# VectorE's score tiles as TensorE tasks of their own, and PV products that no longer wait for a full burst

## The chip, the cores and the metric

One core of one Trainium2 chip. The metric is device microseconds (us) of one execution. Every kernel was timed in several rounds beside the kernel before on the same chip, so a ratio compares runs of the same rounds. The granted TensorE clock differed from run to run. "Clock" below is always this granted share of full speed.

## The reference, cut to what matters

Two transformer layers over 2048 tokens of width 512, each an attention block and an MLP block with residuals. Attention has 32 heads of 16, and its softmax over 2048 keys is most of the work.

```python
B, S, D, H, Dh, F = 1, 2048, 512, 32, 16, 1376
q, k, v = qkv(layernorm(x) @ wqkv)                    # [32 heads, 2048, 16] each
p = softmax((q @ k.T) * Dh ** -0.5, axis=-1)          # 32 x 2048 x 2048
x = x + merge(p @ v) @ wo
x = x + gelu_tanh(layernorm(layernorm(x)) @ w1 + b1) @ w2 + b2
# ... and both lines once more
```

## The kernel before

The program is written by a list scheduler that runs at build time. Every piece of work is a `Task(engine, priority, instructions)`. The scheduler holds a model of when engines and buffers come free and emits each engine's instructions once, in one order. On the chip each engine then runs its own list in that order. Priorities therefore don't exist at run time: only the order and the waits do.

A score tile is 128 keys by 512 queries, in one PSUM bank. Two engines turn scores into weights:

- ScalarE (ACT) takes the exponential of three banks (0 to 2), then of two (3 and 4), and so on in turn.
- VectorE (DVE) takes single tiles in banks 5 (`DLANE`) or 7 (`MISCB`): it evicts the bank to integers whose bits are a rough exponential, makes three shifted copies, and all four images enter the PV product, three of them against pre-scaled copies of V.

Bank 6 (`ACCB`) accumulates PV. A head has 16 channels, so a score matmul uses one of four 32-row groups of TensorE's array (`hp` below). Matmuls in different row groups run side by side (further down, four take 0.39 us together, as long as one). I call a "pass" the time of one matmul, in which up to four such matmuls can run.

This is where a group's scores are sent; the tiles of VectorE (`dts`) join the same burst:

```python
# flow_scores
dts = []
while self.wide and len(grp) + len(dts) < 4:
    d = self.take_d([row groups already used by grp and dts])     # cut
    if d is None:
        break
    dts.append(d)
ops = []
for (sg, j), b in zip(grp, banks):
    ops.append(self.score(sg, j, b))
for sg, j, b, bt, w in dts:
    ops.append(self.score(sg, j, b))
...
yield Task("pe", 0.0, ops)
...                                    # submit the exponential of grp
for d in dts:
    self.d_load(d)                     # submit the eviction

# take_d(hps): a tile in a free row group if there is one
j = next((j for j in sg["todod"] if sg["tiles"][j][1] not in hps), sg["todod"][0])

# score: the row group is in tile_position
e.matmul(self.ps[:, b, ...], lhsT=self.KT[32 * hp:32 * hp + 32, ...],
         rhs=self.QT[32 * hp:32 * hp + 32, ...], tile_position=(32 * hp, 0))
```

PV products wait until a burst is worth its passes, here unless exponential buffers have run out:

```python
# try_pv
value = lambda r: sum(min(r, len(v)) for v in by.values()) / (4.0 * (r + PV_COST))
r = max(range(1, PV_DEEP + 1), key=value)
if value(r) < PV_LEAST and not self.starved and len(near) < sg["n"] - sg["sub"]:
    return
```

Where TensorE would be idle, `fill_pe` puts matmuls on zeros, as many as keep a running activity at `FILL_ACT = 0.62`. They are meant to keep the clock up: with fillers half as wide it was 0.963 to 0.973 (after_fillhalf below). It also sends a single VectorE tile if the gap is long enough, so tiles alone exist before the change too.

## Time and profile before

| | before |
|---|---|
| median of 3 runs (range) | 1710.54 us (1710.01 to 1712.83) |
| span of the profiled run, clock | 1708.6 us, 0.983 |
| ACT busy, idle | 1609.6 us, 99.0 us |
| TensorE matmul busy, idle | 1585.4 us, 123.2 us |
| tiles by ACT / by DVE | 3338 / 758 |
| passes of score matmuls, counted in the order | 1487 |
| filler matmuls of 256 columns | 6152 |

Idle time is the span less the busy time. The lines behind the table are in the prediction. One more of the page is needed later: the chain that ended last, by line, as shares of the span.

### The profile page before, as it was taken

What the parts mean: (1) busy time and instruction counts of PE and PEld (TensorE: products, weight loads), DVE (VectorE), ACT (ScalarE), POOL (GpSimd) and SP (SyncE); (2) the same over time, 40 slices, a digit from 0 to 9 for tenths busy, and PEclk for the clock granted to TensorE, in tenths of its full rate; (3) what the DMA queues carried; (4) which work ended last, traced back from release to release, by engine and by line L of the source; (5) the groups of instructions that cost most, each with busy time, mean ns of one, the idle gap of its engine ahead of it and who ended that gap; (6) DMA issues with size and microseconds to landing.
All of it is one profiled execution on the core that took longest, in us unless ns stands there. A gap on an engine that the chain in (4) does not pass through costs nothing.

```text
span 1708.6 us, 46394 instructions
## 1 busy us (share of the span) xinstructions
PE 1585.4 (93%) x19711; PEld 568.6 (33%) x19711; DVE 1374.4 (80%) x3011; ACT 1609.6 (94%) x1426; POOL 378.5 (22%) x640
## 2 busy tenths in 40 slices
PE   8988999999999999999999998999999999999998
PEld 5222333233223223332223333323232233344444
DVE  6878998859876798768878799886888869887783
ACT  4878999999999999999999999999999999999996
POOL 4045522102211121101212133411011101132220
PEclk9989999999999999999899999999999999999999
DMA  6552000112101120112532230000000100010000
GB/s 167 104 103 69 26 12 8 47 43 59 33 17 41 40 73 14 29 28 69 117 54 54 56 87 18 17 20 11 14 8 8 20 15 5 5 21 7 19 10 14
DMA packets 181259, 66.70 MB, mean 39 GB/s; under 512 B 160859, under 2 KB 175424, under 8 KB 181056
## 3 DMA queue, kind: packets, MB, share of 16 engines
q1 hardware_dynamic: 181056, 63.75, 16.6%
q8 instruction: 158, 2.59, 0.6%
q14 instruction: 45, 0.37, 0.1%
HBM read 19.96 MB, written 15.30 MB: 21 GB/s over the span
## 4 chain that ended last, share of the span: by engine, by line
PE 47%; ACT 40%; DVE 8%; POOL 2%; issue 2%; DMA 1%; SPq 0%; DVEq 0%; POOLq 0%
ACT PT L1110 37%; PE ps L1127 15%; PE ps L1278 13%; PE ps L1035 4%; PE ps L841 4%; PE ps L1397 4%; DVE dp L1195 3%; PE ps L1364 3%; PE ps L1435 3%; ACT h L1427 2%; DVE dp L1223 2%; POOL vs L986 1%; DVE accT L1304 1%; PE ps L1038 1%; ACT L1110 1%
## 5 line engine op out<-in xcount | busy, mean ns | idle before, releaser
L1110 ACT ACTIVATE PT<-ps 128x1536 bf16<-128x1536 f32 (+1 forms) x1348 | 1534.3, 1262 | 67.0 <-PE ps L1127 61.3
L1127 PE MATMUL ps<-QT,KT 32*128 32x512 bf16 (+1 forms) x4608 | 604.2, 363 | 108.5 <-ACT PT L1110 43.8
L1195 DVE TENSOR_SCALAR dp<-ps 128x512 uint16<-128x512 f32 x758 | 510.2, 682 | 208.4 <-PE ps L1127 200.7
L1278 PE MATMUL ps<-PT,V 128*17 128x512 bf16 (+1 forms) x3751 | 469.7, 363 | 0.4 <-DVE accT L1304 0.4
L1223 DVE TENSOR_SCALAR dp<-dp 128x1024 uint16<-128x1024 uint16 (+1 forms) x1170 | 443.2, 422 | 12.7 <-PE ps L1278 8.2
L986 POOL TENSOR_SCALAR vs<-V 128x340 bf16<-128x340 bf16 (+3 forms) x312 | 255.7, 826 | 859.7 <-PE ps L1278 833.1
L1278 PE MATMUL ps<-dp,vs 128*17 128x512 bf16 (+1 forms) x2571 | 397.3, 359 | 0.0
L1127 PEld LDWEIGHTS ps<-QT,KT 32*128 32x128 bf16 x4608 | 163.4, 91 | 637.8 <-issue 173.3
L1035 PE MATMUL ps<-wqkv,zw 128*32 128x256 bf16 x6152 | 241.5, 280 | 1.1 <-DVE accT L1304 1.1
L1278 PE MATMUL ps<-dp,V 128*17 128x512 bf16 (+1 forms) x857 | 201.4, 364 | 3.0 <-DVE accT L1304 2.9
L1035 PEld LDWEIGHTS ps<-wqkv,zw 128*32 128x32 bf16 x6152 | 144.5, 97 | 93.3 <-issue 76.0
L1278 PEld LDWEIGHTS ps<-PT,V 128*17 128x17 bf16 x3751 | 114.7, 88 | 91.1 <-issue 73.7
L1278 PEld LDWEIGHTS ps<-dp,vs 128*17 128x17 bf16 x2571 | 101.9, 89 | 85.3 <-issue 71.4
L1397 PE MATMUL ps<-yT,wf 128*128 128x512 bf16 (+3 forms) x396 | 98.5, 359 | 0.5 <-DVE h L1421 0.3
L841 PE MATMUL ps<-wqkv,xnT 128*128 128x512 bf16 x336 | 94.2, 389 | 2.9 <-DVE dp L862 2.1
L1304 DVE STREAM_TRANSPOSE accT<-ps 128x512 f32<-128x512 f32 (+1 forms) x88 | 58.3, 662 | 24.4 <-PE ps L1278 22.9
L1421 DVE TENSOR_SCALAR h<-ps,b1c 128x512 bf16<-128x512 f32 (+2 forms) x88 | 62.0, 705 | 13.9 <-PE ps L1397 13.5
L1364 PE MATMUL ps<-wo,OT 128*128 128x512 bf16 x240 | 67.4, 383 | 0.2
L1278 PEld LDWEIGHTS ps<-dp,V 128*17 128x17 bf16 x857 | 48.9, 88 | 38.4 <-issue 24.3
L906 POOL TENSOR_TENSOR qt<-n,qy 128x32 f32<-128x32 f32 x32 | 11.1, 347 | 160.1 <-DVE qy L902 159.6
L1344 DVE STREAM_TRANSPOSE OT<-ob 128x512 bf16<-128x512 bf16 (+1 forms) x72 | 46.0, 640 | 0.2
L1397 PEld LDWEIGHTS ps<-yT,wf 128*128 128x128 bf16 (+1 forms) x396 | 29.5, 99 | 46.5 <-issue 18.6
(154 smaller groups left out, 820.1 us busy)
## 6 DMA issues: line engine op xcount, KB each, us to landing
wf<-in_B_w_dram SPq DMA_DIRECT2D x90, 128.0 KB, 2.8
q_scr<-qk SPq DMA_DIRECT2D x22, 256.0 KB, 2.1
k_scr<-qk SPq DMA_DIRECT2D x12, 256.0 KB, 2.0
out_dram<-xres SPq DMA_DIRECT2D x16, 128.0 KB, 1.7
v_scr<-vst SPq DMA_DIRECT2D x12, 136.0 KB, 2.0
V<-v_scr SPq DMA_DIRECT2D x8, 204.0 KB, 4.5
wqkv<-in_A_wqkv_dram SPq DMA_DIRECT2D x3, 512.0 KB, 3.9
q_scr<-h SPq DMA_DIRECT2D x6, 256.0 KB, 2.1
```

What stands on the lines that cost most here:

```text
L841: yield Task("pe", prio, [I(lambda e, c=c: e.matmul(self.ps[:, b, :], lhsT=xnT[:, c, :], rhs=self.wqkv[:, c, which * 512:which * 512 + 512 ...
L986: yield Task("pool", 0.8, [I(lambda e, k=k: e.tensor_scalar(out=self.vs[:, q, k - 1, i:i + n, :], in0=src, scalar1=WSHIFT[k], scalar2=None ...
L1035: P.op("pe", lambda e, p=p: e.matmul(self.ps[p:p + 32, b, 0:w], lhsT=self.zw[:, 0:32], rhs=rhs[:, 0:w], start=st, stop=st, skip_group_chec ...
L1110: S_.submit(Task("act", 1e-5 * gi, [I(lambda e, pt=pt, n=n, b0=b0: e.activation(out=self.PT[:, pt:pt + n, :], in_=self.ps[:, b0:b0 + n, :] ...
L1127: return [I(lambda e, kb=kb, i=i: e.matmul(self.ps[:, b, i * W:(i + 1) * W], lhsT=self.KT[32 * hp:32 * hp + 32, hg, kb * 128:(kb + 1) * 12 ...
L1195: self.S_.submit(Task("dve", 0.0, [I(lambda e: e.tensor_scalar(out=self.dp[:, u, w * 512:(w + 1) * 512], in0=self.ps[:, b, :], scalar1=BIT ...
L1223: yield Task("dve", pr, [I(lambda e, k=k, v=v: e.tensor_scalar(out=self.dp[:, v, 0:N], in0=self.dp[:, u, 0:N], scalar1=float(SHIFT[k]), sc ...
L1278: ops.append((i, I(lambda e, hp=hp, v=v, ap=ap[:, i * W:(i + 1) * W], first=first and i == 0, W=W: e.matmul(self.ps[32 * hp:32 * hp + 17, ...
L1304: yield Task("dve", 0.3, [I(lambda e: e.transpose(self.accT[:, a, 0:W], self.ps[:, ACCB, 0:W]), [("ps", ACCB)], [RA], 0.15 + 0.53 * W / 512)])
L1364: yield Task("pe", pr, [I(lambda e, hg=hg, i=i, b=b: e.matmul(self.ps[:, b, :], lhsT=self.OT[:, hg, i * 128:(i + 1) * 128], rhs=self.wo[:, ...
L1397: yield Task("pe", pr, [I(lambda e, c=c: e.matmul(self.ps[0:M, b, off:off + W], lhsT=self.w1(fc, c), rhs=self.yT[:, c, 0:W], start=(c == 0 ...
L1421: S_.submit(Task("dve", pr - 0.7, [I(lambda e, fc=fc, M=M, b=b: e.tensor_scalar(out=hv[0:M, fc * W:(fc + 1) * W], in0=self.ps[0:M, b, 0:W] ...
```

## The change

The intent: a VectorE tile should not have to wait for an ACT group, and VectorE should get one whenever it is about to run out of work; PV products that wait for partners should go if TensorE has nothing else. The diff, cut to its core:

```diff
+D_IDLE = 1.0
+D_PRIO = 0.5
+PV_IDLE = 0.4
@@ flow_scores
-            for sg, j, b, bt, w in dts:
-                ops.append(self.score(sg, j, b))
+            for d in dts:
+                S_.submit(Task("pe", -0.5, self.score(d[0], d[1], d[2])), cb=lambda d=d: self.d_load(d))
...
-            for d in dts:
-                self.d_load(d)
@@ new
+    def d_solo(self):
+        S_ = self.S_
+        if not self.wide or self.P.free["dve"] - S_.now + sum(o[4] for t in S_.pend["dve"] for o in t.ops) > D_IDLE:
+            return
+        d = self.take_d([])
+        if d is not None:
+            S_.submit(Task("pe", D_PRIO, self.score(d[0], d[1], d[2])), cb=lambda: self.d_load(d))
@@ d_loaded: a timer at the planned end of each eviction calls d_solo
+        heapq.heappush(S_.timers, (self.P.last_writer[("dp", bt["unit"], w)].t1, S_.seq, self.d_solo))
@@ try_pv
             if value(r) < PV_LEAST and not self.starved and len(near) < sg["n"] - sg["sub"]:
-                return
+                t = self.P.drain + PV_IDLE
+                if S_.now < t or self.pv_out:
+                    ...                # set a timer for pv_again, which calls try_pv
+                    return
```

More of the change, by code (lines that the diff above doesn't have):

```diff
@@ L1204, in d_loaded @@
             self.S_.release("mb", b)
+        S_ = self.S_
+        S_.seq += 1
+        heapq.heappush(S_.timers, (self.P.last_writer[("dp", bt["unit"], w)].t1, S_.seq, self.d_solo))
         self.d_ready(bt, 0, bt["unit"], [w])
@@ L1259, in try_pv @@
             if value(r) < PV_LEAST and not self.starved and len(near) < sg["n"] - sg["sub"]:
-                return
+                t = self.P.drain + PV_IDLE
+                if S_.now < t or self.pv_out:
+                    if not self.pv_timer:
+                        self.pv_timer = True
+                        S_.seq += 1
+                        heapq.heappush(S_.timers, (max(t, S_.now) + 0.01, S_.seq, self.pv_again))
+                    return
             pick = [v[k] for k in range(r) for v in by.values() if len(v) > k]
@@ L1284, in try_pv, with pv_again @@
             S_.submit(Task("pe", 1.0, ops), cb=lambda sg=sg, pick=pick: self.pv_done(sg, pick))
+    def pv_again(self):
+        self.pv_timer = False
+        self.try_pv()
     def pv_done(self, sg, pick):
@@ L1531, in build @@
         self.pv_first = False
+        self.pv_timer = False
         self.starved = False
```

## The prediction

> **What bounds the kernel now.** I read the page's busy shares and chain first, then busy time by stage, then the groups by shape, then the waits of ScalarE (ACT). A score tile is a 128x512 block of logits in one PSUM bank. Most go to ACT, which takes the exponential of three or two banks in turn. Some go to VectorE (DVE): it evicts the bank to integers (L1195), makes three shifted copies (L1223), and all four images enter the PV product.
>
> ```profile
> PE 1585.4 (93%) x19711; PEld 568.6 (33%) x19711; DVE 1374.4 (80%) x3011; ACT 1609.6 (94%) x1426; POOL 378.5 (22%) x640
> ...
> PE 47%; ACT 40%; DVE 8%; POOL 2%; issue 2%; DMA 1%; SPq 0%; DVEq 0%; POOLq 0%
> ```
>
> PE and ACT both look full. But PE's 93% holds filler matmuls on zeros (L1035), and TensorE's ends are modelled. The stages separate them:
>
> ```profile
> core 0: us, PE busy (x) PEld busy (x) DVE busy (x) ACT busy (x) POOL busy (x), PEclk, DMA share, GB/s
> 0.00:200.00 200.00, 177.07 (x1813) 68.05 (x1816) 154.79 (x366) 155.63 (x158) 86.52 (x238) 0.94 0.45 100
> 200.00:1600.00 1400.00, 1309.02 (x16314) 450.08 (x16306) 1148.00 (x2478) 1362.79 (x1183) 276.08 (x384) 0.99 0.14 32
> 1600.00:1709.00 109.00, 99.36 (x1600) 50.44 (x1592) 71.57 (x170) 91.20 (x87) 15.86 (x18) 1.00 0.06 13
> ```
>
> For 1400 us ACT works 97.3% of the time: idle is 37 us there, 44 us in the start and 18 us in the tail. What ACT still waits for in the middle is one thing:
>
> ```profile
> ACT PT L1110 <- PE ps L1127: 31.8, 85, 1.8
> ```
>
> That is 85 short waits for score matmuls, 0.37 us each. So the kernel is ACT-bound, and time is bought by taking tiles from ACT without making it wait longer. The shapes give the price of a tile, the DVE side and the filler:
>
> ```profile
> L1110 ACT ACTIVATE PT<-ps 128x1536 bf16<-128x1536 f32 x642 | 953.9, 1486 | 43.2 <-PE ps L1127 38.2
> L1110 ACT ACTIVATE PT<-ps 128x1024 bf16<-128x1024 f32 x706 | 743.8, 1059 | 23.8 <-PE ps L1127 23.1
> L1195 DVE TENSOR_SCALAR dp<-ps 128x512 uint16<-128x512 f32 x758 | 510.2, 682 | 208.4 <-PE ps L1127 200.7
> L1223 DVE TENSOR_SCALAR dp<-dp 128x1024 uint16<-128x1024 uint16 x1104 | 427.7, 429 | 12.5 <-PE ps L1278 8.2
> L1035 PE MATMUL ps<-wqkv,zw 128*32 128x256 bf16 x6152 | 241.5, 280 | 1.1 <-DVE accT L1304 1.1
> ```
>
> One more bank costs ACT 1486 - 1059 = 427 ns. DVE is idle 208 us ahead of its evictions, nearly all of it waiting for a score matmul: that is the idle time the change goes after.
>
> **What the Trainium skill says.** "ScalarE: Activation LUTs", section "What ACT_TABLE_LOAD costs": an ACTIVATE with immediate operands is 186 ns plus 0.833 ns per column, and neighbours overlap by about 93 ns. 512 columns are 427 ns; the trace agrees. The two forms sum to 1697.7 us but cover 1534.3 us together, an overlap of 121 ns per instruction, so one instruction's fixed cost is 1059 - 854 - 121 = 84 ns.
> "TensorEngine Tiling (Array Packing)", section "Key Properties": changing the tiling mode drains TensorE. In the timeline, bursts inside one mode start 0.22 us apart (802.88 to 803.10), across modes 0.32 us (804.39 to 804.71): a switch costs about 0.1 us.
> "PSUM — Partial Sum Buffer", section "Engine vs sequencer instructions": ACT and DVE queues are strict FIFO and matmuls start and end in program order. The trace agrees, painfully, just after the kernel widens to five banks:
>
> ```profile
> 108.29 0.41 DVE L782 TENSOR_SCALAR xn<-xres,mv,rs 128x512 bf16<-128x512 bf16 x1 [7.16 <-DMA xnT<-xn]
> ...
> 109.74 1.03 PE L1127 MATMUL ps<-QT,KT 32*128 32x512 bf16 x4 [6.94 <-DVE dp L1195]
> ...
> 110.87 2.54 ACT L1110 ACTIVATE PT<-ps 128x1536 bf16<-128x1536 f32 x2 [6.23 <-PE ps L1127]
> ```
>
> A late DMA held DVE, the bank DVE had not emptied held PE, and PE starved ACT.
>
> **The change, part by part.** The scheduler runs at build time, so I compared the two instruction orders. DMA and GpSimd counts are equal. ACT loses 13 of the 1536-wide and 14 of the 1024-wide exponentials and gains one of 512: 3338 tiles become 3272. DVE evictions go from 758 to 824, wide shifts from 1104 to 1215, narrow ones from 66 to 42. By units of eight head groups the gain is 13 tiles at most (92 to 105) and 1 to 10 in the others, so it is spread over the middle.
>
> ACT: 66 tiles x 0.427 = 28.2 us, plus 26 fewer instructions x 0.084 = 2.2 us: 30.4 us less. All of it lies on the bounding engine.
>
> DVE: 66 x 0.673 (510.2/758) = 44 us, 111 x 0.387 (427.7/1104) = 43 us, less 24 x 0.26 = 6 us: busy 1374 to about 1455 us, 87% of a 1680 us span. It fits into the 208 us of idle time and is off the bounding path.
>
> PE: each tile that moves needs four PV products in place of one: 198 more tile products, four at a time in the 0.22 us of the timeline, about 11 us. Score passes: for each run of adjacent score matmuls I took the longest queue on one 32-row group. That gives 1487 passes before and 1887 after. The old code put a DVE tile into the ACT group's burst and chose a free row group; a solo tile has no such choice or stands alone. 400 x 0.22 = 88 us more. PV passes count 1762 before and 1827 after, 65 x 0.22 = 14 us, so the smaller bursts waste little beyond the 11 us. Mode switches rise from 2687 to 2798, 111 x 0.1 = 11 us. Fillers of this kind fall from 6152 to 4432, 430 passes of four x 0.11 (256 columns, half a pass) = 47 us less. Net PE work: 88 + 14 + 11 - 47 = +66 us, in a span that should be 30 us shorter. It lies beside ACT's work as long as each ACT group finds its banks written in time, but the slack goes: filler (1538 x 0.11 = 169) plus idle (1708.6 - 1585.4 = 123) is about 292 us before and roughly 292 - 113 - 30 = 149 us after.
>
> PV while idle: PV never bounds ACT directly in this trace (no listed ACT wait names it); earlier products free exponential buffers sooner. I count nothing for it.
>
> Sum with ACT idle unchanged: 1710.5 - 30.4 = 1680.1 us.
>
> **Rivals.**
> (1) PE becomes the co-bound. With half its slack gone, more groups come late. For: solo tiles stand ahead of PV in priority, the tiles taken with a group now even ahead of that group, and I count 135 runs of score matmuls that open with a tile in a DVE bank ahead of an ACT group, against 63 before; in such a run a late DVE holds ACT up at once. Against: groups still outrank everything but those tiles, the new code no longer makes a group wait for DVE's bank to be planned free, and ACT has 1.0 to 1.4 us of other banks to chew on. If the 85 waits doubled, 32 us come back: about 1710, no gain at all. I expect about a tenth of that.
> (2) ACT's idle time shrinks. PE's score matmuls wait 29.2 us on DVE evictions in the middle; if decoupling removes a third of ACT's 32 us and the 6.2 us stall at 110 us, the result is near 1664. Against: that stall starts from a late DMA that the change does not touch, and the changed order still has DVE wait there for the same kind of transfer and PE wait for several.
> (3) DVE becomes the bound. At 87% with FIFO waits it would show as later eviction and fewer free banks. Against: the scheduler stops giving it tiles when it has over 1.3 us queued. It would make the time about 1690.
> (4) Fewer fillers let the clock fall. Granted clock is 0.99 in the middle; real work replaces the fillers, so I expect no change.
>
> **Range and chances.** From 1680 I add 2 us for rival 1 in part offset by 2: 1682 us, 1.7% under 1710.5. The range takes ACT idle from 8 us less to 14 us more: 1672 to 1694. The line for faster by 2% is 1676.3 us; it needs the full tile saving and 4 us less idle: 0.24. Slower by 2% needs over 64 us of new waits: 0.01. Within 2%: 0.75.
>
> **What would show it right or wrong.** Right: exponentials 1503 to 1505 us busy on the page, DVE near 1455, ACT busy near 1579 and ACT idle within 10 us of 99, most of it still in the first 200 us; fillers 4432. Step by step: if ACT busy falls by 30 but the span by less, the wait list must show ACT waiting for score matmuls for much more than 61 us over the whole span, and rival 1 (PE waits on evictions grow) or 3 is read from what those matmuls waited for. If the span falls by over 34 us, those waits must be well under 61 us. The prediction is wrong in kind if ACT is under 96% busy between 200 and 1570 us, or the granted clock there falls under 0.97.

## More of the kernel before

L1110 is the exponential, L1127 the score matmul, L1278 the PV product, L1035 the filler.

```profile
ACT PT L1110 37%; PE ps L1127 15%; PE ps L1278 13%; PE ps L1035 4%; PE ps L841 4%; PE ps L1397 4%; DVE dp L1195 3%; PE ps L1364 3%; PE ps L1435 3%; ACT h L1427 2%; DVE dp L1223 2%; POOL vs L986 1%; DVE accT L1304 1%; PE ps L1038 1%; ACT L1110 1%
```

The chain runs through ACT's exponentials for 37% of the span and through TensorE's score and PV work for 28%.

## The result, and the profile after

| | before | after |
|---|---|---|
| median, range | 1710.28 us (1708.60 to 1712.83) | 1694.92 us (1691.75 to 1697.68) |
| ratio (95%) | | 0.9908 (0.9884 to 0.9933) |
| profiled span, clock | 1708.6, 0.983 | 1695.3, 0.988 |
| ACT busy / idle | 1609.6 / 99.0 | 1580.9 / 114.4 |
| DVE busy | 1374.4 | 1456.1 |
| TensorE busy / idle | 1585.4 / 123.2 | 1618.0 / 77.3 |

A ratio here and below is the mean time of one kernel's runs over that of the other's of the same rounds, so it is not quite the ratio of the medians quoted. The change gains 0.9%: within 2%, as expected, but little more than half of the 28.5 us predicted, and the median lies 0.9 us above the predicted range.

First the page of the kernel after: busy time by engine, then the chain that ended last by engine and by line. L1113 is now the exponential, L1128 the score matmul, L1297 the PV product.

```profile
PE 1618.0 (95%) x18235; PEld 543.4 (32%) x18235; DVE 1456.1 (86%) x3164; ACT 1580.9 (93%) x1400; POOL 384.0 (23%) x640
...
PE 60%; ACT 30%; DVE 6%; DMA 2%; issue 1%; SPq 1%; POOL 0%; DVEq 0%; POOLq 0%
ACT PT L1113 27%; PE ps L1128 22%; PE ps L1297 17%; PE ps L844 4%; PE ps L1420 4%; PE ps L1458 4%; PE ps L1038 4%; PE ps L1387 3%; DVE dp L1205 2%; DVE dp L1236 2%; ACT h L1450 2%; PE ps L1041 1%; DMA yT<-xn 1%; DVE accT L1327 1%; DMA xnT<-xn 0%
```

The arithmetic of tiles came true: ACT works 28.7 us less. But the chain, which was 47% TensorE and 40% ACT, is now 60% and 30%, with score matmuls up from 15% to 22%. Busy shares alone hardly show this: TensorE goes from 93% to 95%.

The stages of the kernel after (columns as in the prediction's table of stages):

```profile
0.00:200.00 200.00, 181.82 (x1896) 69.93 (x1900) 161.03 (x371) 158.81 (x162) 87.24 (x241) 0.97 0.47 100
200.00:1590.00 1390.00, 1335.89 (x14879) 422.44 (x14868) 1222.62 (x2627) 1335.63 (x1157) 281.68 (x383) 0.99 0.14 33
1590.00:1695.30 105.30, 100.27 (x1469) 51.01 (x1467) 72.43 (x169) 86.41 (x83) 15.09 (x16) 0.99 0.04 12
```

In the middle ACT was busy for 97.3% and is for 96.1%: 54 us idle where 37 us were. Start and tail are as before (41 and 19 us idle). So the lost gain is in the middle. ACT's waits for score matmuls there, then TensorE's largest waits over the whole span, all in the kernel after (us in total, times, longest):

```profile
ACT PT L1113 <- PE ps L1128: 48.7, 78, 5.6
```
```profile
PE ps L1128 <- ACT PT L1113: 21.3, 76, 0.9
PE ps L1128 <- DVE dp L1205: 17.1, 22, 6.3
```

and TensorE's in the kernel before:

```profile
PE ps L1127 <- ACT PT L1110: 43.8, 133, 1.0
PE ps L1127 <- DVE dp L1195: 43.2, 69, 6.9
```

ACT waits more for TensorE (31.8 to 48.7 us in the middle), and TensorE waits less for ACT and for DVE, half or under half as long. An engine that others wait for longer while it waits less itself is the one short of time. Most of its lateness is then not a bank that is still full, but other work in front. That is a reading; the experiments have to test it.

What is that work? The score matmuls by shape, before and after; the number after the bar is busy time, and the idle time just before them follows.

```profile
L1127 PE MATMUL ps<-QT,KT 32*128 32x512 bf16 x3584 | 530.4, 389 | 97.9 <-ACT PT L1110 39.3 <-DVE dp L1195 38.5 <-DVE QT L969 2.8
```
```profile
L1128 PE MATMUL ps<-QT,KT 32*128 32x512 bf16 x3584 | 591.5, 384 | 49.2 <-ACT PT L1113 19.7 <-DVE dp L1205 15.6 <-DVE mv L773 2.3
```

The same 3584 matmuls of the same size keep TensorE busy for 61 us more; with the 1024 narrower ones it is 74 us (604.2 to 678.4). One matmul isn't longer (389 and 384 ns): fewer run side by side. The timeline shows it. A run of four score matmuls in the kernel before:

```profile
607.80 0.39 PE L1127 MATMUL ps<-QT,KT 32*128 32x512 bf16 x4
```

and in the kernel after, a run of four and the exponential that it released (start, duration, count, idle time before it):

```profile
604.57 0.61 PE L1128 MATMUL ps<-QT,KT 32*128 32x512 bf16 x4
605.06 7.09 ACT L1113 ACTIVATE PT<-ps 128x1536 bf16<-128x1536 f32 x6 [0.26 <-PE ps L1128]
...
606.51 0.60 PE L1128 MATMUL ps<-QT,KT 32*128 32x512 bf16 x4
```

Four in 0.39 us is one pass in four row groups; four in 0.6 us is two passes: one of the tiles shares a row group with another.

Where do the 400 added passes come from? Mostly not from tiles that stand alone. Counted over the two emitted orders, the runs of score matmuls without any ACT tile rise only from 13 to 67, while the passes that VectorE's tiles add to runs with ACT tiles rise from 122 to 489. Both kernels take 498 tiles together with a group and choose a row group that is free in it. Before, all of them stand in the burst of that group. After, as tasks of their own, 389 of them are emitted earlier, behind the group *before*, with whose row groups nobody compared them. These make about 340 of the 400 passes; the run at 604.57 us above is one, by its place in the order, while the one at 606.51 us holds a solo tile.

### The profile page after: what moved, and what is told of

Its sections match the earlier page's. It is cut to its first block, busy times and chain, and to the rows that moved or that the text cites. A ratio compares the mean times of both kernels' runs of the same rounds, so it can differ in the third digit from the quotient of the medians.

```text
span 1695.3 us, 43536 instructions
## 1 busy us (share of the span) xinstructions
PE 1618.0 (95%) x18235; PEld 543.4 (32%) x18235; DVE 1456.1 (86%) x3164; ACT 1580.9 (93%) x1400; POOL 384.0 (23%) x640
## 4 chain that ended last, share of the span: by engine, by line
PE 60%; ACT 30%; DVE 6%; DMA 2%; issue 1%; SPq 1%; POOL 0%; DVEq 0%; POOLq 0%
ACT PT L1113 27%; PE ps L1128 22%; PE ps L1297 17%; PE ps L844 4%; PE ps L1420 4%; PE ps L1458 4%; PE ps L1038 4%; PE ps L1387 3%; DVE dp L1205 2%; DVE dp L1236 2%; ACT h L1450 2%; PE ps L1041 1%; DMA yT<-xn 1%; DVE accT L1327 1%; DMA xnT<-xn 0%
## 5 line engine op out<-in xcount | busy, mean ns | idle before, releaser
L1113 ACT ACTIVATE PT<-ps 128x1024 bf16<-128x1024 f32 (+1 forms) x1322 | 1505.8, 1256 | 81.6 <-PE ps L1128 75.8
L1128 PE MATMUL ps<-QT,KT 32*128 32x512 bf16 (+1 forms) x4608 | 678.4, 359 | 53.1 <-ACT PT L1113 21.3
L1205 DVE TENSOR_SCALAR dp<-ps 128x512 uint16<-128x512 f32 x824 | 557.8, 684 | 121.2 <-PE ps L1128 114.0
L1236 DVE TENSOR_SCALAR dp<-dp 128x1024 uint16<-128x1024 uint16 (+1 forms) x1257 | 490.4, 432 | 10.9 <-PE ps L1297 6.6
L1297 PE MATMUL ps<-PT,V 128*17 128x512 bf16 (+1 forms) x3674 | 472.0, 361 | 0.2 <-DVE accT L1327 0.2
L1297 PE MATMUL ps<-dp,vs 128*17 128x512 bf16 (+1 forms) x2802 | 408.2, 357 | 0.4 <-DVE dp L1236 0.4
L1128 PEld LDWEIGHTS ps<-QT,KT 32*128 32x128 bf16 x4608 | 178.5, 91 | 578.7 <-issue 172.5
L1297 PE MATMUL ps<-dp,V 128*17 128x512 bf16 (+1 forms) x934 | 195.7, 358 | 2.4 <-DVE accT L1327 2.2
L1038 PE MATMUL ps<-wqkv,zw 128*32 128x256 bf16 x4432 | 188.2, 275 | 0.8 <-DVE accT L1327 0.8
L1297 PEld LDWEIGHTS ps<-PT,V 128*17 128x17 bf16 x3674 | 111.3, 88 | 114.9 <-issue 102.2
L1297 PEld LDWEIGHTS ps<-dp,vs 128*17 128x17 bf16 x2802 | 102.4, 89 | 111.2 <-issue 95.3
L1038 PEld LDWEIGHTS ps<-wqkv,zw 128*32 128x32 bf16 x4432 | 105.8, 96 | 80.3 <-issue 60.8
L1420 PE MATMUL ps<-yT,wf 128*128 128x512 bf16 (+3 forms) x396 | 104.8, 369 | 4.8 <-DMA yT<-xn 3.9
L1297 PEld LDWEIGHTS ps<-dp,V 128*17 128x17 bf16 x934 | 48.1, 88 | 43.4 <-issue 26.7
L1420 PEld LDWEIGHTS ps<-yT,wf 128*128 128x128 bf16 (+1 forms) x396 | 28.5, 100 | 59.2 <-issue 30.1
L972 DVE TENSOR_SCALAR QT<-qraw,scl,qbias 128x512 bf16<-128x512 bf16 (+1 forms) x87 | 37.3, 431 | 10.3 <-DMA qraw<-q_scr 10.0
```

Source lines behind the costliest of these rows:

```text
L1038: P.op("pe", lambda e, p=p: e.matmul(self.ps[p:p + 32, b, 0:w], lhsT=self.zw[:, 0:32], rhs=rhs[:, 0:w], start=st, stop=st, skip_group_chec ...
L1113: S_.submit(Task("act", 1e-5 * gi, [I(lambda e, pt=pt, n=n, b0=b0: e.activation(out=self.PT[:, pt:pt + n, :], in_=self.ps[:, b0:b0 + n, :] ...
L1128: return [I(lambda e, kb=kb, i=i: e.matmul(self.ps[:, b, i * W:(i + 1) * W], lhsT=self.KT[32 * hp:32 * hp + 32, hg, kb * 128:(kb + 1) * 12 ...
L1205: self.S_.submit(Task("dve", 0.0, [I(lambda e: e.tensor_scalar(out=self.dp[:, u, w * 512:(w + 1) * 512], in0=self.ps[:, b, :], scalar1=BIT ...
L1236: yield Task("dve", pr, [I(lambda e, k=k, v=v: e.tensor_scalar(out=self.dp[:, v, 0:N], in0=self.dp[:, u, 0:N], scalar1=float(SHIFT[k]), sc ...
L1297: ops.append((i, I(lambda e, hp=hp, v=v, ap=ap[:, i * W:(i + 1) * W], first=first and i == 0, W=W: e.matmul(self.ps[32 * hp:32 * hp + 17, ...
```

## The experiments

Most kernels are timed in three rounds. Besides the ratio I give the time "at one clock". Within one kernel the time follows the clock of the run: the 29 distinct timed runs of the kernel before go from 1702.9 us (0.988) to 1714.9 us (0.978). A fit over all 106 runs, one level per kernel and one slope for all, gives 12.2 us per 0.01 of clock (standard error 0.4, scatter 1.4 us). At a clock of 0.985 it puts the kernel before at 1707.4 and the changed one at 1698.8 us. This is an association, as a stall can lower the clock too, and for a kernel that only ran at another clock it is an extrapolation.

### The halves alone

**d_only** leaves out the PV half.

```diff
@@ changed kernel, try_pv
-                t = self.P.drain + PV_IDLE
-                ...
-                    return
+                return
```

> Only the VectorE half of the change (own TensorE tasks, solo tiles); the PV rule is that of before. The instruction order holds 3280 exponential tiles (58 fewer than before, worth 58 x 0.427 + 23 x 0.084 = 26.7 us of ScalarE). Theory late transfers: what came back was a handful of stalls behind DMA transfers that land later than planned, so ScalarE idle time is between the 99 us of before and the 114 us of the changed kernel by accident of the order, and each long ScalarE stall traces to a DMA wait: 1684 to 1699 us. Theory crowded TensorE: score passes are 1870 here against 1487, so idle grows as in the whole change, spread over many short waits: 1697 to 1700 us, with the short waits (up to 0.6 us) clearly above the 20 us of before.

Measured: 1719.01 us (1710.02 to 1720.35), ratio 1.0062 (1.0034 to 1.0090). ACT has 3280 tiles and is busy for 1587.5 us, 22 us less than before, and the kernel is still slower: ACT's idle time went from 99 to 121 us. So moving tiles this way costs more than it saves unless the PV half is there. Neither theory had expected so much (1684 to 1700 us).

**pv_only** adds the PV half to the kernel before (the same lines as in the diff of the change, and nothing else).

> Only the PV half (a short burst may go when TensorE has been idle), on the kernel before. 3322 exponential tiles, 16 fewer: 7.3 us of ScalarE. Score passes 1506, so TensorE is hardly more crowded. Theory crowded TensorE: no idle growth, 1703 us. Theory late transfers: 1703 us too, plus or minus what its own order hits, some 8 us; any ScalarE stall over 2 us must trace to a DMA wait.

Measured: 1706.58 us (1704.91 to 1711.59), ratio 0.9989 (0.9961 to 1.0017): nothing by itself. The halves don't add up: together they gain 0.9%, separately they lose 0.6% and gain 0.1%.

### Are the waits accidents of late transfers?

A first theory was that the new stalls were transfers which the plan believes to land sooner than they do. Planning a transfer to take 4 us in place of 2 moves everything that uses it later.

```diff
@@ both kernels: after_lat4 and before_lat4
-            op.t1 = op.t0 + dur + (2.0 if lat is None else lat)
+            op.t1 = op.t0 + dur + (4.0 if lat is None else lat)
```

> The changed kernel with one number altered: the build-time plan takes a transfer to land 4.0 us after its issue in place of 2.0 us, so the TensorE and VectorE instructions that need it are placed later in their queues. 3268 exponential tiles against 3272. Theory late transfers: ScalarE idle falls from 114 us to about 98 us or less, long stalls in the middle go, about 1680 us. Theory crowded TensorE: score passes are the same (1886), so nothing is gained, 1691 to 1698 us.

> The same altered number in the kernel before, as the control. 3347 exponential tiles, 9 more: 4.2 us more ScalarE work. Theory late transfers: the 6.2 us stall at 110 us and some of the stalls near 820 us go, idle 99 falls to about 88 us: about 1704 us. If nothing is gained it is 1714 us.

Measured: after_lat4 1697.51 us, ratio 0.9945 (0.9904 to 0.9986), no better than the change as it is; before_lat4 1729.50 us, ratio 1.0116 (1.0092 to 1.0140), worse than the 1714 us expected at worst. The theory found no support.

One stall of the changed kernel is a transfer, though. At the border of two stages (core time 867 to 881 us) the timeline of the kernel after shows, first in the DMA queue and then on the engines:

```profile
843.78 14.85 SPq L997 DMA_TRANSPOSE KT<-k_scr  x7
858.73 9.00 SPq L999 DMA_DIRECT2D V<-v_scr  x7
```
```profile
872.02 5.43 SPq L960 DMA_TRANSPOSE qraw<-q_scr  x3
...
875.84 0.41 DVE L972 TENSOR_SCALAR QT<-qraw,scl,qbias 128x512 bf16<-128x512 bf16 x1 [8.64 <-DMA qraw<-q_scr]
...
876.91 0.71 PE L1128 MATMUL ps<-QT,KT 32*128 32x512 bf16 x3 [6.35 <-DVE dp L1205]
...
877.66 1.02 ACT L1113 ACTIVATE PT<-ps 128x1024 bf16<-128x1024 f32 x1 [5.55 <-PE ps L1128]
...
878.51 1.89 PE L1387 MATMUL ps<-wo,OT 128*128 128x512 bf16 x4
```

Read it upwards. ACT lost 5.55 us to a score matmul, that one waited 6.35 us for a bank that DVE had not emptied, DVE stood for 8.64 us before a Q tile whose transfer the queue only took up after 24 us of K and V loads. In the stretch of 4 us after 878 us the granted clock was 0.57, and the four matmuls of the last line took 1.89 us. **after_kprio** and **before_kprio** let the K and V loads of the later head groups go behind the Q loads:

```diff
-                       [("kscr", tt) for tt in range(12)], [...], 1.4, 2.6)
+                       [("kscr", tt) for tt in range(12)], [...], 1.4 if hg < 2 else 1.6 + 0.01 * hg, 2.6)
@@ and the same priority for the V load
```

> The changed kernel; only the order of the layer-3 loads in the DMA queue differs: K and V of head groups 0 and 1 first, the other six after the Q rows. Theory layer boundary: about 8 us of the 15 us that came back are two ScalarE stalls at 878 and 881 us, behind Q rows that stood after eight K and eight V loads in the queue. Then these stalls go, ScalarE idle falls from 114 to about 106 us, and with 3267 exponential tiles (5 fewer, 2 us) the time is about 1685 us, ratio to before near 0.985. If the stall only moves elsewhere: 1693 us, ratio 0.990.

> Control: the same reordering in the kernel before. All four engines have the very same instruction order as before; only 24 lines of the DMA queue differ. The kernel before has no stall over 1 us at the boundary (0.8 us at 871 us), so nothing is to be gained: 1709 us, ratio 1.000, within 0.3%.

Measured: after_kprio 1693.47 us (1688.35 to 1697.26), ratio 0.9912 (0.9879 to 0.9944); before_kprio 1706.78 us, ratio 0.9995 (0.9967 to 1.0022). The stall at 877 us is gone, but between 800 and 1100 us ACT's idle time is 26.3 us against 21.8 with it: others took its place. Over the whole span it fell only from 114.4 to 111.0 us. The border is a true cost of a few us in this order of instructions, not the 15 us that are missing. (Two more stalls of the changed kernel begin with a transfer: TensorE waited for `yT<-xn`, 1.9 us at 515 us and 2.0 us at 1523 us. In after_kprio neither TensorE nor DVE waits over 1.6 us for a transfer in the middle, and ACT's idle time is hardly less.)

### Fillers, and the place of the tiles in the order

**fill_more** raises the filler. If TensorE has slack and the clock was short, it should gain.

```diff
-FILL_ACT = 0.62
+FILL_ACT = 0.80
```

> The changed kernel with the fillers' target for TensorE activity at 0.80 in place of 0.62: 5447 filler matmuls in place of 4808, 3260 exponential tiles in place of 3272 (5 us). Theory clock: the stalls are long because fewer fillers let the clock fall; then the mean granted clock rises above 0.989, ScalarE idle falls by 5 to 10 us more than a DMA accident explains, and the time is about 1682 us. Theory layer boundary: the fillers do nothing for it, clock and idle stay, the time follows the tiles: about 1690 us.

**d_behind** was meant to put the tiles that are taken with a group behind the group, where they can't hold it up. My rival 1 in the prediction named exactly this.

```diff
-                S_.submit(Task("pe", -0.5, ...
+                S_.submit(Task("pe", 0.01, ...
```

> The changed kernel, except that a VectorE tile taken with a ScalarE group goes to TensorE behind that group (priority 0.01) and not ahead of it (-0.5). 3275 exponential tiles, 1 us more. Theory crowded TensorE, as recorded as rival 1: a late VectorE then no longer holds the group up, the short ScalarE waits fall, about 1685 us. If these waits were never the cost: 1694 us plus or minus 5, with short waits (up to 0.6 us) still near 21 us.

Measured: fill_more, with 5447 filler matmuls of all kinds in place of 4808, 1711.94 us (1705.97 to 1724.53), ratio 1.0031 (0.9979 to 1.0083): the gain is gone, and the clock didn't rise (0.973 to 0.987). d_behind 1707.34 us, ratio 0.9999 (0.9955 to 1.0043): the gain is gone there too. Its passes are nearly the same (1877 for 1887), and ACT's idle time was 125.6 us. But the edit did not do what it was meant to do: in the emitted order 385 of the 494 tiles taken with a group still stand behind the group before, as 389 of 498 do in the changed kernel. So this run doesn't test rival 1; it shows that two orders with the same passes can lie 0.9% apart.

### Which engine's work costs time: the halves of work

Now the theory from the waits: TensorE is short of time, and what costs is score passes that no longer share. The rival: DVE's added 82 us of work. Up to here the edits changed the order itself (before_kprio only that of the DMA queue), and d_only, before_lat4, fill_more and d_behind all came out 8 us or more slower than anything written down beforehand: a new order brings stalls of its own. Each of the next kernels therefore keeps the order of instructions of its parent and makes one kind of instruction half as wide. Their outputs are wrong, which doesn't matter for the times. Each edit is also made in the kernel before, as a control, because taking work away may help any kernel.

**after_shhalf** and **before_shhalf**: DVE's shifted copies on half of the columns (once the whole of a buffer has been written).

```diff
+            M = N // 2 if (v, n) in self.seen else N
+            self.seen.add((v, n))
-            ... self.dp[:, v, 0:N], in0=self.dp[:, u, 0:N] ...
+            ... self.dp[:, v, 0:M], in0=self.dp[:, u, 0:M] ...
```

> Wrong result on purpose: the changed kernel with the same instruction order on TensorE, ScalarE, GpSimd and the DMA queue, but VectorE's shifts write half their columns (after the first use of a buffer): about 1200 x 0.19 = 230 us less VectorE work. Theory late VectorE: evictions come sooner, TensorE is held less, ScalarE idle falls from 114 us to under 100 us: under 1681 us. If VectorE's load was not the cause: 1691 us or more.

> Control, wrong result on purpose: the same halving in the kernel before, about 210 us less VectorE work. VectorE was idle 20% of the time already: theory late VectorE expects a small gain, 1704 to 1709 us; an equal gain in both kernels says that VectorE's load is no part of the difference.

**after_pvhalf** and **before_pvhalf**: the PV products of the three pre-scaled images on half of the columns; by the count of passes 68 and 63 us of TensorE work.

```diff
-                    ... ap=ap[:, i * W:(i + 1) * W] ..., W=W
+                    ... ap=ap[:, i * W:i * W + (W // 2 if sh else W)] ..., W=(W // 2 if sh else W)
```

> Wrong result on purpose: the changed kernel with every instruction in the same place on all engines, but the PV matmuls of the three shifted images stream half their columns. TensorE work falls by (2142 + 660/2) / 4 x 0.11 = 68 us, about what the change added (66 us). ScalarE work is the same, 1581 us. Theory crowded TensorE: lateness came from TensorE's lost slack, so ScalarE idle falls from 114 us back to 99 us or less: 1680 us or less. Theory late DMA and VectorE: the stalls start on a transfer or on VectorE, so idle stays at 108 us or more: 1689 us or more, or worse if the clock falls.

> Control, wrong result on purpose: the same halving in the kernel before, (1977 + 594/2) / 4 x 0.11 = 63 us less TensorE work, same order. Theory crowded TensorE: this kernel still had its slack, so little is gained: 1704 to 1709 us. If it gains as much as the changed kernel does, the change did not make TensorE the cause.

**after_dhalf** and **before_dhalf**: the score matmuls of VectorE's tiles on half of the columns. A tile that shares its pass with a whole one saves nothing; one that has a pass to itself saves half a pass. Counted over the order, in units of whole passes, 1887 become 1608.5 in the changed kernel (61 us at the 0.22 us that bursts are apart in the prediction) and 1487 become 1417 in the kernel before (15 us). Put in tiles: 557 of 824 tiles have a pass to themselves after, 140 of 758 before.

```diff
     def score(self, sg, j, b):
+        H = 2 if b in (DLANE, MISCB) and self.wide else 1
-        ... self.ps[:, b, i * W:(i + 1) * W] ... rhs=self.QT[..., 0:W]
+        ... self.ps[:, b, i * W:i * W + W // H] ... rhs=self.QT[..., 0:W // H]
```

> Wrong result on purpose: the changed kernel, same order on every engine, but the score matmuls of VectorE's tiles stream half their columns. Score passes fall from 1887 to 1608.5, 61 us of TensorE work, because these tiles had passes of their own. Theory extra passes: about 12 us come back at equal clock (0.2 us per us of TensorE work, from the PV halving): 1687 us at clock 0.985. If the passes were free (done while TensorE waited anyway): at most 3 us, 1696 us.

> Control, wrong result on purpose: the same halving in the kernel before, where these tiles mostly share a pass with the ScalarE group: passes fall only from 1487 to 1417, 15 us of TensorE work. Theory extra passes: 2 to 3 us gained, 1704 us at clock 0.985. If it gains as much as the changed kernel, the gain is not that of the passes.

| | median us (range) | ratio to before (95%) | ACT idle us | at one clock |
|---|---|---|---|---|
| the change | 1694.92 (1691.75 to 1697.68) | 0.9908 (0.9884 to 0.9933) | 114.4 | 1698.8 |
| after_shhalf | 1691.71 (1687.32 to 1695.79) | 0.9899 (0.9861 to 0.9938) | 110.0 | 1694.1 |
| before_shhalf | 1707.99 (1704.38 to 1714.08) | 1.0002 (0.9968 to 1.0036) | 97.5 | 1705.3 |
| after_pvhalf | 1692.99 (1687.43 to 1709.84) | 0.9944 (0.9881 to 1.0006) | 107.2 | 1686.1 |
| before_pvhalf | 1700.72 (1698.13 to 1704.34) | 0.9957 (0.9927 to 0.9988) | 94.2 | 1697.0 |
| after_dhalf | 1677.22 (1676.32 to 1681.38) | 0.9814 (0.9775 to 0.9852) | 99.7 | 1679.3 |
| before_dhalf | 1705.13 (1701.06 to 1713.13) | 0.9977 (0.9937 to 1.0018) | 90.9 | 1704.3 |

DVE's load isn't the cause: 147 us less of it (1456.1 to 1308.6 us busy) brings nothing that the intervals can tell. The score passes do cost time: with half of the width of VectorE's score matmuls gone the time is 1677 us (1687 had been expected) and ACT's idle time 99.7 us, about the 99.0 us of the kernel before. The control's idle time fell too, to 90.9 us, but that page is from the fastest of its runs. The times are the safer comparison: with these matmuls halved in both kernels, in the same rounds, the change gains 27.9 us (1705.13 to 1677.22), nearly the 28.5 us predicted, where it gains 15.4 us at full width. So most of what is missing goes with the width of these matmuls; from the three ratios and their intervals I estimate 12 us, give or take 10. The page of after_dhalf, its chain and its waits (L1129 is the score matmul here):

```profile
PE 1571.2 (94%) x18235; PEld 546.7 (33%) x18235; DVE 1452.2 (87%) x3164; ACT 1576.3 (94%) x1400; POOL 383.0 (23%) x640
...
ACT 54%; PE 36%; DVE 6%; DMA 2%; issue 1%; SPq 1%; DVEq 0%; POOLq 0%; POOL 0%
```
```profile
ACT PT L1113 <- PE ps L1129: 63.3, 94, 8.5
```
```profile
PE ps L1129 <- ACT PT L1113: 46.1, 154, 1.0
```

The chain turns round, from 60% TensorE and 30% ACT to 36% and 54% (in the control 42% and 45%, in the kernel before 47% and 40%). ACT waits 63.3 us for score matmuls over the whole span (75.8 after, 61.3 before), and TensorE waits 46.1 us for ACT again (21.3 after, 43.8 before).

How much does a microsecond of such work cost? From the change to after_dhalf the ratio falls by 0.0094, of 1708.6 us that is 16.1 us for 61 us of passes: 0.26. The control falls by 0.0023, 3.9 us for 15 us: 0.26 as well, though its interval includes no effect. That the two agree so well is luck at this noise: by the fall of TensorE's busy time on the pages, 47 and 26 us, the rates are 0.34 and 0.15. Whether the kernel before pays the same rate, and only had few such passes, is not shown.

The PV halves say less, and by what was written down beforehand they went against the theory: after_pvhalf was to have 99 us of ACT idle time or less and has 107.2, and the control was to gain little and gained at least as much. before_pvhalf gains 0.43% for 63 us, a rate near 0.12. after_pvhalf ran at clocks from 0.983 down to 0.967, and its interval is too wide to tell it from the change; at one clock it would be 13 us faster, and the control 10 us. So at one clock both kernels gain alike from less PV work, which fits TensorE's work costing something in both, and says nothing about the difference between them. The clock of the changed kernel fell with this work taken away (0.967 to 0.983, against 0.986 to 0.990), so that part of what one gains goes there.

### The other way round: adding work, and taking fillers

**before_pvplus** adds TensorE work to the kernel before, whose order stays: in front of each PV product of a pre-scaled image, the same product on half of its columns (wrong; by the count of passes 63 us).

```diff
-                    ... e.matmul(self.ps[32 * hp:32 * hp + 17, ACCB, 0:W], lhsT=v, rhs=ap, ...)
+                    ... [e.matmul(self.ps[32 * hp:32 * hp + 17, ACCB, 0:w], lhsT=v, rhs=ap[:, 0:w], ...) for w in ((W // 2, W) if sh else (W,))][-1]
```

> The kernel before, same order, each PV matmul of a shifted image preceded by a half-wide copy of itself that adds into the sums (wrong result on purpose): (1977 + 594/2) / 4 x 0.11 = 63 us more TensorE work, what the change adds (66 us net). Theory TensorE work costs at this margin: 11 us or more lost at equal clock, 1718 us or more at clock 0.985, the size of what came back. If added TensorE work lies beside ScalarE's, as the prediction said: 1707 to 1709 us.

**solo_only** puts the tiles taken with a group back into its burst, and keeps `d_solo` and the PV half.

```diff
-            for d in dts:
-                S_.submit(Task("pe", -0.5, ...
+            for sg, j, b, bt, w in dts:
+                ops.append(self.score(sg, j, b))
...
+            for d in dts:
+                self.d_load(d)
```

> The changed kernel, but tiles taken with a ScalarE group are put into the group's burst as before; only the solo tiles and the PV rule are new. 3303 exponential tiles (35 fewer than before: 16.1 us of ScalarE) and 1565 score passes (17 us more TensorE work than before). Theory extra passes: idle grows by 5 us, so about 1696 us at clock 0.985, ahead of the changed kernel's 1699 although it takes half as many tiles from ScalarE. Theory solo tiles are to blame: idle grows by 15 us as in the change, 1706 us.

**after_fillhalf** makes the changed kernel's fillers half as wide, at the same places (the result is right).

```diff
-    ... self.ps[p:p + 32, b, 0:w] ... rhs=rhs[:, 0:w]
+    ... self.ps[p:p + 32, b, 0:w // 2] ... rhs=rhs[:, 0:w // 2]
```

> The changed kernel, same order everywhere, correct result, but each filler matmul on zeros streams half its columns: 4432 / 4 x 0.055 = 61 us less TensorE work. Theory fillers are slack (as the prediction counted them): no gain at equal clock, 1699 us at clock 0.985, and a lower clock makes the raw time worse. Theory fillers take their turn in the queue: 10 to 20 us gained at equal clock, about 1684 us; the raw time then depends on how far the clock falls (12.5 us per 0.01).

**kp_f45** is an attempt at a better kernel: after_kprio with less filler from the start (`FILL_ACT = 0.45`).

> Candidate: the changed kernel with the K and V loads reordered (as in after_kprio) and the fillers' activity target at 0.45 in place of 0.62: 2879 fillers in place of 5015 (59 us less), 3268 exponential tiles against 3267. Theory fillers take their turn: below after_kprio's 1693 us at equal clock by 10 us or so; if the clock falls by 0.01 the raw time is even, 1693 us, else about 1685 us. Theory fillers are slack: 1693 us at equal clock and worse in raw time.

Measured: before_pvplus 1780.57 us (1777.27 to 1784.84), ratio 1.0414 (1.0379 to 1.0449). TensorE's busy time rose by 89 us and the time by 71 us (0.0414 x 1708.6), more than the nominal 63:

```profile
PE 1674.3 (94%) x22282; PEld 707.7 (40%) x22282; DVE 1377.9 (78%) x3011; ACT 1626.2 (92%) x1426; POOL 378.0 (21%) x640
...
PE 69%; ACT 18%; DVE 9%; issue 2%; POOL 1%; DMA 1%; SPq 0%; DVEq 0%; POOLq 0%
```

So this addition found no room beside ACT's work, in the kernel before already. The rate is not a constant: low when work is taken away, about one when 63 us are added inside PV bursts. The two edits also differ in kind: a halved matmul stays one instruction, while each of the 2571 copies brings a weight load of its own (568.6 to 707.7 us). The 123 us of idle and 170 us of filler in the kernel before did not absorb the addition.

solo_only 1704.46 us (1697.53 to 1706.94), ratio 0.9961 (0.9924 to 0.9998). It has only 1565 passes, but keeps less of the gain in tiles (3303 on ACT). The theory of the passes had expected 1696 us and its rival, that solo tiles are to blame, 1706: by its number this run lies with the rival. Two stalls of the border kind, at 879 and 884 us, cost it 8.5 us, which would be the difference; that they are an accident of this order is not shown. What it does show is which part makes the passes: with the solo tiles kept and the other tiles back in their bursts, 78 of the 400 are left.

after_fillhalf 1706.78 us (1704.73 to 1713.24), ratio 0.9994 (0.9971 to 1.0016). All of the gain is gone, at clocks of 0.973 to 0.963 where the change's profiled run had 0.988. At one clock it would be at 1688.7 us, 10 us better, but this is extrapolated far beyond the clocks that it ran at. kp_f45 1695.64 us (1691.36 to 1701.46), ratio 0.9914 (0.9895 to 0.9932) at clocks near 0.975: even with the change. So less filler went with a lower clock and brought no gain. That the fillers themselves cost time in the queue rests on the extrapolation alone. I found no version that clearly beats the changed kernel.

## Why the prediction was wrong

The direction was right, and so was "within 2%"; the time fell just outside the range, 13 us above the number. By its own steps:

- **ACT's gain: right.** 66 tiles and 26 instructions were to take 30.4 us; ACT's busy time fell by 28.7. Exponentials were to end at 1503 to 1505 us, and the group reads 1505.8:

```profile
L1113 ACT ACTIVATE PT<-ps 128x1024 bf16<-128x1024 f32 (+1 forms) x1322 | 1505.8, 1256 | 81.6 <-PE ps L1128 75.8
```

- **DVE: right.** "about 1455" was 1456.1, and rival 3 did not happen: a tenth of DVE's work can go without an effect that the intervals show.
- **Rival 4 (clock): right for the middle (0.99 in both), with 4432 fillers as counted.** Over the whole run the clock rose from 0.983 to 0.988. By the fit that is worth 6 us, so part of the 15.4 us gained may come with the clock and not from ACT's saving, which the prediction did not foresee: at one clock the gain is 8.6 us.
- **TensorE's added work: right in kind, too large in size.** The prediction said net +66 us. The page shows score matmuls +74 us (88 predicted), PV products +8 (1068.4 to 1075.9, summed over the three groups; 14 predicted, and 11 for mode switches, which have no line of their own), the counted fillers -53 (-47), and TensorE's total +33 us. The count of 1887 passes is right, but its reason, "a solo tile has no such choice or stands alone", explains the lesser part: about 340 of the 400 come from tiles that did choose a free row group, and then stood in another burst than the one they chose it for.
- **What that work costs: the step that failed.** "It lies beside ACT's work as long as each ACT group finds its banks written in time, but the slack goes". The sum charged it 2 us, after "I expect about a tenth of that" in rival 1, with fillers and idle time counted as 292 us of slack. The measured rate is about 0.26 us per us of unshared passes in the changed kernel (the control can't tell it from zero). An estimate from the prediction's own 66 us is 66 x 0.26 = 17 us, and 1680.1 + 17 = 1697 us against 1694.9 measured. With the page's figures the estimate is softer: 0.26 of the real work (74 + 8) is 21 us, and of TensorE's net 33 us it is 9 us, depending on what a removed filler gives back. The direct evidence doesn't need the rate: halve these matmuls and ACT's idle time falls from 114.4 to 99.7 us, where the prediction assumed 99.0, and the time to 1677 us; halve them in both kernels and the change gains 27.9 us.
- **Why the error could be seen beforehand.** The first fence of the prediction shows the chain with TensorE at 47% and ACT at 40%. I set it aside for the busy share of ACT in the middle, and took TensorE's idle time as a reserve. Idle moments of an engine that runs one list in order are only in part a reserve for work that stands elsewhere in the list: at a rate of 0.26 three quarters of the passes did hide, and in before_pvplus little or nothing did.
- **Rival 1's mechanism: not what the trace shows.** It expected TensorE to wait more for DVE's evictions and tiles ahead of a group to hold it up. The waits for evictions fell from 43.2 to 17.1 us. Whether a tile ahead of a group holds it up was not tested, because d_behind left the tiles where they were. TensorE was co-bound, as the rival's name says, through its own work.
- **"I count nothing for" the PV half: wrong in company.** Alone it does nothing (0.9989), but without it the other half is 0.6% slower than before where both together are 0.9% faster. That PV products now use moments in which TensorE would stand is the likely reason; it is argued, no run separates it.
- **ACT's idle time "within 10 us of 99": wrong**, 114.4. The test "wrong in kind if ACT is under 96% busy between 200 and 1570 us" was very near: 1315.7 of 1370 us, 96.0%.

What stays open: the short waits (up to 0.6 us) of ACT in the middle are alike in both kernels (21 us in sum in each), and the listed long ones grew from 9 to 14 (11 to 28 us). So in the trace what came back is long stalls, while after_dhalf gets most of its gain there from short waits (13 us are left, and 24 us of long ones): it makes up for the stalls more than it removes them. Four of the long stalls, 14 us in sum (at 518, 877, 881 and 1526 us), follow waits for transfers of 8.6 us on DVE and 3.9 us on TensorE, where the kernel before has no such wait over 1.2 us in its middle. Which of the long ones follow from the passes and which are accidents of this one order can't be told one by one: after_dhalf keeps these late transfers (7.7 and 2.9 us) and still has the idle time of before, after_kprio is nearly free of them and has 26 us of other long stalls. And the rate's rise from 0.26 to about one is shown for two kinds of work only. A version that compares a tile's row group with the burst in which it will really stand was not tried.

## What to carry to other kernels

Before you unbundle work, count what shares a pass: a tile in a free row group of a burst adds no pass, and one that stands alone or doubles a row group adds one. A free place must be chosen against the burst that the tile ends up in, so look at the order that comes out and not at the intent. Read the shares of the chain and who waits less than before, not the busy share of one engine; an in-order engine at 93% can limit the time, and its fillers and gaps can't be counted as slack in full. Here two orders with nearly the same passes lay 12 us apart, so tests that keep the order say more. When effects are near 1%, note the granted clock of each run, and halve a suspected cost in place in both kernels.

## What the Trainium skill lacked or had wrong

- "Perfetto Trace Analysis", section "Identifying the Most-Contended Engine", says to judge TensorE's headroom not by matmul busy time but by useful work against peak and by the busy share of weight loads. Here the weight loads fell from 568.6 to 543.4 us (33% to 32%) while TensorE's share of the chain rose (47% to 60%) and its own waits shrank. Most of that fall is the fillers' weight loads (144.5 to 105.8 us); those of the score matmuls rose (163.4 to 178.5 us). Useful work against peak was not computed here.
- "TensorE: Matmul & The Clock Gate", section "Part 1: The HAM clock gate", calls the warm-up penalty under 1% of a typical span, and the page's "Terms" price throttled time for TensorE itself. Neither says what the mean granted clock is worth in a long kernel in which ACT works beside it: here 12 us per 0.01 between runs of one program (0.7% from 0.988 to 0.978).
- The same page, section "Part 3: Packing small matmuls — row/col tiling", tells what tiles in different row groups gain. It doesn't state what two neighbours in one row group lose: a run of four took 0.60 us in place of 0.39 us, and the change added 400 such passes.
- None of the pages that I used puts a price on TensorE work that lies beside a busy ScalarE: about 0.26 us per us of unshared score passes in the changed kernel, and 71 us for a nominal 63 us that were added to PV bursts.
